# Interleaved memory attention and ReGLU: loads of two weights gated, first MLP products of two tiles joined, turns of P in either tiling

## The chip, the cores and the metric

The kernel runs on one core of one Trainium2 chip. The metric is device time in microseconds of one execution. An execution is also recorded by the hardware profiler; its own time is given beside the span that the trace shows.

## The reference, cut to what matters

Two layers, each an attention with recurrent memory and then an MLP, both added to x, both on a layer norm of x. The attention goes through 64 segments of 32 tokens in order; the first 8 rows of each segment's result are the memory that the next segment sees.

```python
def _A_ref(x, mem0, Wq, Wk, Wv, Wo, seg_len):      # S 2048, D 448, H 16, Dh 256, M 8, seg 32
    mem = mem0
    for s in range(n_seg):
        h = jnp.concatenate([mem, xs], axis=1)      # 8 rows of memory, 32 tokens
        q, k, v = h @ Wq, h @ Wk, h @ Wv            # per head
        scores = q @ k.T * scale, masked
        p = _softmax(scores, axis=-1)
        o = (p @ v) @ Wo
        mem = o[:, :M, :]
        outs.append(o[:, M:, :])
def _B_ref(x, W_gate, W_up, W_down):                # F 1792
    gate = x @ W_gate
    return (gate * (gate > 0) * (x @ W_up)) @ W_down
x = x + _A_ref(_layernorm(x), ...)
x = x + _B_ref(_layernorm(x), ...)
# the same two lines once more, with the same weights
```

## The kernel before, in words

**Folded weights.** At the start the kernel turns Wq, Wk and Wv on TensorE (`transposes`, L742 and L747) and multiplies them (`product`, L761): A holds Wq times Wk for every head, Bsb holds Wv times Wo. From then on scores are h A h and outputs are (p h) B, so no q, k or v is formed. `weights` loads Wq and Wk in four groups of heads, each group into half of eight staging slots, and behind them in the program all of Wv and Wo (`load(self.Wv_d, ...)` and the copies to `Wos`). Wv is staged in slots 8 to 15; Wo is parked in buffers that are free at the start, among them YT, hG, Ug and G2. The first two steps of the chain (`unfused`, L1039 and L1062) use Wv and Wo directly, since B isn't ready.

**The chain.** `chain(step)` is the recurrent part: the 8 memory rows of one segment of layer one and, seven steps later, of layer two, 70 steps in all. A step has products with A (L934, eight tiles of the array), scores (L1128), softmax, the turn of P, the product of P with the rows of h, called Y (L1185 and L1188), the products with B (L973, four column tiles), and a turn of the result into mT (the `Sel` products). `middle` holds scores to Y. Its probabilities P lie in Pm; those of eight-row pieces of an even tile of layer two, which ride along with the chain (66 turns), lie in Pr.

**The tiles.** The 16 tiles of 128 tokens go through `att_group` four heads at a time: products with A (L1274, two row tiles), scores (L1300), softmax, two turns of P (from Px), Y in two row tiles, and the output products (L451, untiled). That is 16 tiles in layer one and the 8 odd ones in layer two, four groups each, 96 groups. Y results wait in YT, two blocks used by turns. The MLP of a tile is `glu_units`: the first products for gate and up together (L1372), two row tiles with 64 rows each, 14 chunks of 128 hidden columns times 7 pieces of 64 rows, 128 tokens as moving columns. Gate and up stand in different PSUM banks; ScalarE writes the ReLU to hG (L1377), VectorE multiplies with up (L1378). `glu_down` makes the second products (L451, untiled) from hG, of which there is one block.

**A turn of P** before is one untiled transposition (`packed`, called in `middle` and `pt`): 128×128 in bf16 to one PSUM bank, one eviction to PT (104 rows; 128 columns in the chain, 256 for a group's two turns).

**What sets the order.** `_Sched` gives every operation an engine, a cost and a priority, and finds each one's waits. TensorE's order is fixed by the string LINE (`line`); ORDER shifts priorities of units (`part`). An operation has a mode, which is the tiling of the array: 0 untiled, 1 four column tiles, 2 two row tiles, 3 two column tiles, 4 eight tiles. An operation with `also` may take a second mode, and `line` then picks the one that its neighbours have. `room` and `alias` say which earlier users of a buffer have to be done. PSUM has eight banks in two pools. All DMAs are issued by SyncE's queue in order. Where TensorE would idle, `filler` puts spare products (L1406).

`tiles` runs at every fourth step: groups of tile t in layer one, the MLP of tile t, the MLP of tile t−4 in layer two, and groups of layer two.

Of the kernel before, what the change touches and what calls it, by code (L numbers as in the profile page):

```python
# [8 lines left out]
ALU = mybir.AluOpType  # L9
# [3 lines left out]
D = 448  # L13
# [19 lines left out]
ORDER = ("AkAPMPZMEsWPzkVtwAm0YgdLXFCHdymsALTpcTXKWNMRKLt0H0AgHAG0gihNl0bCLbZBRyVqwoWAgOvEFplk0ptQ0orawUuaBIdaABka0AA0aa"  # L33
         "UaWkSa0fNaChwaA0kcaaXrwSQNQolVYPjLmRRyjDqc0uzbiwvY0gEaaatIahC0NHXvgHbX0qAhiALw0iY0xVfRVDkaUymAt0AaAYaeCfRWpXfR"
         "lJxhempFZBlhCipGXOTk0eOorF0OaAa0faVtHTAdPi0SgiUZl0Nm0FmTRpXckrAguNAAk0TxnnA0HxlDgNSEoEVUlUXDaSSAHiaEFaPPSQjusW"
         "YsHcogi0CaBoAdNDtXVPMQkFMca0pUUVDgiUJ0xagIaPQboIbArY0SqePoFsAwfZKMgAmQsVlzU0HCASKQgeTRjtIFHqamOut0D0ya0nLcrAeT"
         "qrItxafza0hRCbp0ClsrvyAbvP0nD0EOIc0PZVUvetwAYKgbvL0w0KalaAOavpQIi0oAA0ZoAYlwmSPsLHUKDArMgzAgUELIXQA0LdqAnU0duA"
         "RSfhqzjm0kXOhRXJVfMAtVaKbaPYaKxc0G0ZSzTNpcOgMoKsBXiXfRmvsXAophduABSMYerUaaYlanAPrjhwGfrKHNc0WWgiNONAY0ZjIihT0V"
         "t0QqJhnS0LcxVbFjWBImEg0GMxNQjpxcpwkS0I0aYzavtOoz00gKAX0cLJkCaCWwVoVlVNmZ0jObxAFx00DReqAnTgacYaA0VBQTGgvXdZNTGn"
         "ixZZaanneAvXk0qXyH0tAXRAocegRGeXokpA0bAxdEZoHCsFcPcys0oFa0raAmeZcEyZQprpBkgUf00mVmuQAL0tfAtAILpMjffkzbZy0UJaXD"  # L40
         "aDgXWPdp0AXdVewhBXaIvATytDudIpyJxp0XTUswAFVsNGsiaRpOZz0ZRPojkrzZQnAfLhuKvaKXa0yCmDasEGHmoHFQXN0bYLZLTJDiANQTbR"
         "BwmtqZMtPAyNaPhavEUjupByVrFRkoAjhqSSfsUwC0AXoNBSmwAPyyXOpAcrWU0SeRJ0EpypIhQsmOFtmBji0vczampgaOqCxa0Zj0AAYMaaaa"
         "aavRbLKjCaaaaaaaaaaaaaaaaaaawkgqnN0IaIleHbO0")

SIGNS = "ABCDEFGHIJKLMNOPQRSTUVWXYZabcdefghijklmnopqrstuvwxyz0123456789+-*/=<>()[]{}.,:;!"
LINE = ("AFGEENLEGEEEFEEEMIIFGFEEFFMEM~UIJHEEEEAEDGAGECCCCCECABIIICFBECCBBKJCDCEDCBCBJJIECFDDBBJMrBIMNIAEBCECCACADBaaCC"
        "TPAnCCASCAQhAPDAONAgMBAKBAAHbHCGADaACCAAHIAVAYGBADOADCLCADJOFAHOEONEFGEBACCFBBCAAAAWAAAKARAAHOdHASAZAQXEAAAB~D"
        "AK~BAffDAC=CbAEAYEDW5WWWAAETADDRQAAANAAAKKKAJJAIAHHABFAADACAAAAAAAMSYYBAKdKbKAMR~JXAMLA~NAAAEEAHDAaaFFCCGCUABB"
        "RACPAANNNOAALANwMA1LJCJIICLHHHAGJIAAEFLAADCCAAAAABABAMAAXXQHJAaIIAQAVAAASDFDACDCbbFABADCAETAAXRABPBANNNAALANM4"
        "4MKRArKIIIBHHHAGAIHeAADEAACBBFAAAABCAATMBAXWdWKAaKhJALWuALbKAAAEJEUADDA55ElECG0ABBxBwAdCBssstAEApArqDOCAmkBBKQ"  # L50
        "hmAfVe+eeeCIdcAdcHCQAFAVVAGZAARAPIOhENNNANALMALLKcAaDIAAPGBaFZBEEEFAACKEPyxW~QEUEtAGAAPoBsnA~BDCkkkAAiiDADCgfA"
        "ADAbABBXdAAVAUAXTTTATzSBBwRQCBAAMARAAJDIAHHHKAHGBSGGdAFOTZPgOAADATNBXNBfLBBBRFFBEAAF))GqpFA/BBlF9=A8L777AA5AI5"
        "5BtBiF0AA4yDvAAttcCrrrAagEEA=FlkFlkDDhZngNACCcAbCaaaBZbAbaBFAEAVAAEQXRAPWPcDDNNNAALNKK-+aZK7ADA+4Vl2DMCzzzFAAI"
        "wvUETDssACApACtABBjADhAAfCBEcccAcAaABaZCvBWAVAAZASuSlsARRRBCAANAbhAAKAAsriiWJBBUHHAFPAREAAaABRfBL1LBBBFFBIEB))"
        "HSGACCAF+BBB7ACe4B7A222FbAAyAxzynewCAcCBGpguoTGFRkEQiiiESEEeAVcDccD7ibjAAZYsYDXXXBWABHWVHAlTAQAWgAPANUNpCMMMAA"
        "KMDIAH44UDTC0GAQA2wDD~KuTDssstAAqYEApoEDlMAAiADmAfDCdAADaaaAAYABAYXAAAUSxpZTARsRCBBANNNOAALAYACIAAGBRWdGFAPYOE"
        "AAATNBYBWgLBBBbIBEAAH{]MCCC>}RCADC-BEA8hE666AA4A55AbA2AAyCy3BwwedCVArrrGqFsrEeADPmDjDDoiRDffDKUcccfAAbaEaaHBBB"
        "VHATZAKAQAEDVNTNNNAALA//AIABGH7NG5AA3KRA000QJyACwzyDTCSuAKApDvpANnm!CCkkkAEAhDDAFAAbccDDAAAXAAVAUTnTTTATqiECBB"
        "OBAAAAYelAjXKAAIIkASRATGAACACSNCWMBdBBBFFBOEHAA))SGpF=CCCAE9LA7oDD4445AA2AA0E10ZygxAAeXtks:CvAqqqIgFBEAkADlkCF"
        "iCLmCdeCKcEaDCGXXXABVAXXUAUABSAABGOASNTMaMMMAAUJJJKQ77ff5D+AA2GB0AAyyyDAAvAxwAAKJsYpAAoHBMlk>CBiiijEAAfAAAAedA"  # L60
        "aCABBWWAAATYAStSSSAphBAAOBcAooDaAAkdApoAWvWuZJVVhHBGHGRAQPFAAACNaABMttLBBBFFJBEEBAC76DnmDAHBiy4BBwBY~LAtkDCqqq"
        "~CqVpCAAonEECkAAoBhgNAeDKcccAAbaIAaZAXOBVHFcZLSGAQqFPPPAHDMDZLNMGbKDJAAAGLTGZBFFFAAGACAAwwCVCLsFABBoCCBqEkAJii"
        "iAIPCeAgfBBbA[aaDAeAXBBVAUUUAASARTSqpZSAtQBPAOAAMMMNAAKAAdWrBBGGSmSdGGAZPFBQBDaTODNACCCGGCFCHT][ITHq<ADA*HAB=A"
        "8K7778AJA4A54dlBBA6ayAAwAvultttwuAAbrFpaoFponBFEkqEEE8hoElgYjHeeeGdfFeeE,AmHDYgZDDXPDaEUTaDWSSSAXRAYY-vEPdWAAU"
        "DMSOCQQQAERANAMDCNNAAAKIAAHFAEEADDDUADCAQBAUcGTGGRHAGBADRAEADDGAAJBOBCCBEAADCAAAAAACAAADAAAABAAAAAA")
# [1465 lines left out]
```

## Time and profile before

| | |
|---|---|
| median of 3 runs | 1504.0 us (1503.89 to 1506.61) |
| the profiled execution | 1502.79 us |
| its span | 1501.0 us |
| granted clock, mean | 0.999 |
| POOL busy | 171.7 us (11%) |
| PEld (weight loads) busy | 1059.1 us (71%) |

The span runs from the first to the last instruction of the program in the trace. PE is TensorE's products, PEld its weight loads, which overlap with them. A row of the lines view reads: line, engine, operation, what it writes and reads, shape, count | busy us, mean ns of one | idle before it and what ended that. A row of the timeline reads: start us, us, engine, line, operation, what, shape, count. Products of TensorE are pipelined, so the printed lengths overlap; the time between the starts of two rows is what the first one costs.

### The profile page before, as it was taken

To read this page: it belongs to the slowest core of one execution; us is meant where nothing else is said; L and a number is where in the kernel's file an instruction comes from. 1 tells how busy PE (TensorE), PEld (TensorE's weight loads), DVE (VectorE), ACT (ScalarE), POOL (GpSimd) and SP (SyncE) were. 2 spreads that over 40 slices of the span, in tenths; PEclk is the share of its full clock that TensorE was granted. 3 is DMA by queue.
4 is the path that set the end of the run, shared out by engine and by line. 5 is a ranking of instruction groups with operands and counts; after the bars stand their busy time and mean duration, and the time that the engine had idled before them with its cause. 6 is when DMAs were issued, how large, how long until landed. Compare 5 with 4: busy or idle time off the path is not lost.

```text
span 1501.0 us, 83432 instructions
## 1 busy us (share of the span) xinstructions
PE 1482.8 (99%) x37128; PEld 1059.1 (71%) x37128; DVE 1144.8 (76%) x3528; ACT 909.7 (61%) x2539; POOL 171.7 (11%) x669
## 2 busy tenths in 40 slices
PE   8999999999999999999999999999999999999999
PEld 6557566676767777777768677777768776677776
DVE  6657678787777878688878877688777877778765
ACT  6776566666666666555565656565665665565543
POOL 3010111111111111011110111011110011111000
PEclk9999999999999999999999999999999999999999
DMA  9602100000000000000000000000000000000000
GB/s 231 184 25 66 54 7 12 11 9 8 9 4 12 11 8 15 4 17 6 17 6 12 11 9 14 3 18 5 18 5 8 14 9 14 4 10 6 12 5 15
DMA packets 62262, 34.12 MB, mean 23 GB/s; under 512 B 31552, under 2 KB 61776, under 8 KB 61904
## 3 DMA queue, kind: packets, MB, share of 16 engines
q1 hardware_dynamic: 61904, 28.80, 8.1%
q8 instruction: 292, 4.78, 1.4%
q14 instruction: 66, 0.54, 0.1%
HBM read 21.36 MB, written 1.84 MB: 15 GB/s over the span
## 4 chain that ended last, share of the span: by engine, by line
PE 94%; DVE 2%; ACT 1%; DMA 1%; issue 1%; SPq 0%; POOL 0%; DVEq 0%
PE psG L451 24%; PE psG L1274 17%; PE psG L1372 12%; PE psC L973 11%; PE psC L934 9%; PE psG L934 4%; PE psG L1185 3%; PE psG L761 3%; PE psG L1300 2%; PE psC L451 2%; PE psC L1128 2%; PE psC L1185 1%; PE psG L973 1%; PE psG L1188 1%; DMA Bsb<-in_A_Wq_dram 1%
## 5 line engine op out<-in xcount | busy, mean ns | idle before, releaser
L1274 PE MATMUL psG<-HT,A 64*128 64x128 bf16 x4980 | 288.9, 216 | 1.2 <-issue 1.2
L451 PE MATMUL psG<-Bsb,YT 128*128 128x448 bf16 x1288 | 274.6, 352 | 0.0
L1274 PE MATMUL psG<-HX,A 64*128 64x128 bf16 x3735 | 269.6, 216 | 0.5 <-issue 0.3
L1274 PEld LDWEIGHTS psG<-HT,A 64*128 64x128 bf16 x4980 | 236.5, 94 | 13.6 <-issue 4.2
L441 ACT ACTIVATE Ug<-psG 64x128 bf16<-64x128 f32 (+2 forms) x442 | 156.6, 374 | 68.5 <-PE psG L1274 56.6
L1274 PEld LDWEIGHTS psG<-HX,A 64*128 64x128 bf16 x3735 | 195.5, 94 | 0.8 <-issue 0.8
L1372 PE MATMUL psG<-G,glu 64*128 64x128 bf16 x5950 | 190.7, 216 | 1.2 <-issue 0.9
L1372 PEld LDWEIGHTS psG<-G,glu 64*128 64x128 bf16 x5950 | 175.4, 94 | 13.6 <-issue 6.2
L451 PEld LDWEIGHTS psG<-Bsb,YT 128*128 128x128 bf16 x1288 | 113.0, 97 | 95.7 <-issue 10.0
L973 PE MATMUL psC<-Bsb,YTm 128*32 128x448 bf16 x3416 | 172.9, 353 | 0.4
L1112 DVE STREAM_TRANSPOSE uT<-Usb 128x384 bf16<-128x384 bf16 x280 | 154.0, 551 | 0.8
L934 PE MATMUL psG<-A,mT 64*32 64x448 bf16 x4032 | 152.5, 350 | 0.0
L934 PE MATMUL psC<-A,mT 64*32 64x448 bf16 x3808 | 147.3, 350 | 0.5 <-ACT mT L441 0.5
L973 PEld LDWEIGHTS psC<-Bsb,YTm 128*32 128x32 bf16 x3416 | 85.5, 97 | 67.0 <-DVE YTm L444 1.6
L441 ACT ACTIVATE YT<-psG 128x448 bf16<-128x448 f32 x233 | 118.8, 543 | 10.6 <-PE psG L1188 9.1
L444 DVE CAST Ug<-psG 64x128 bf16<-64x128 f32 (+2 forms) x254 | 108.1, 438 | 16.9 <-PE psG L1274 12.9
L934 PEld LDWEIGHTS psC<-A,mT 64*32 64x32 bf16 x3808 | 76.0, 92 | 53.4 <-ACT mT L441 5.2
L1377 ACT ACTIVATE hG<-psG 128x512 bf16<-128x512 f32 (+1 forms) x127 | 69.0, 543 | 63.2 <-PE psG L1372 58.0
L451 PE MATMUL psG<-glu,hG 128*128 128x448 bf16 x448 | 99.3, 352 | 0.0
L934 PEld LDWEIGHTS psG<-A,mT 64*32 64x32 bf16 x4032 | 80.1, 92 | 19.8 <-DVE mT L444 0.7
L1378 DVE TENSOR_TENSOR hG<-hG,psG 128x512 bf16<-128x512 bf16 (+1 forms) x116 | 70.5, 613 | 29.2 <-ACT hG L1377 28.3
L444 DVE CAST YT<-psG 128x448 bf16<-128x448 f32 x136 | 82.0, 616 | 9.5 <-PE psG L1188 8.1
(235 smaller groups left out, 2856.9 us busy)
## 6 DMA issues: line engine op xcount, KB each, us to landing
HR<-xn SPq DMA_DIRECT2D x128, 32.0 KB
Tsb<-Rsb SPq DMA_DIRECT2D x256, 1.5 KB
Tsb<-Rsb SPq DMA_DIRECT2D x256, 2.0 KB
Bsb<-in_A_Wk_dram SPq DMA_DIRECT2D x6, 448.0 KB
Bsb<-in_A_Wq_dram SPq DMA_DIRECT2D x6, 448.0 KB
HR<-Rsb SPq DMA_DIRECT2D x126, 1.5 KB
HR<-Rsb SPq DMA_DIRECT2D x126, 2.0 KB
X<-in_A_x_dram SPq DMA_DIRECT2D x16, 112.0 KB
```

The source lines that it names most:

```text
L441: return E.activation(out, i, ACT.Copy, scale=1.0 if scale is None else scale)
L444: return E.tensor_copy(out, i)
L451: return E.matmul(out, lhsT=lhsT, rhs=rhs, **k)
L761: i = E.matmul(bk.ap()[row0:row0 + mn, to:to + of.stop - of.start], lhsT=lhs[:, et, m0:m0 + mn], rhs=rhs[:, et, of], start=(et == 0), stop ...
L934: i = E.matmul(ub[v].ap()[32 * j:32 * j + 32, 0:D], lhsT=self.mT[rw, WHERE[b], first:first + 32], rhs=cols, start=(b == 0), stop=(b == 6), ...
L973: x = E.matmul(bo.ap()[32 * j:32 * j + 32, 0:D], lhsT=self.YTm[:, q, :], rhs=self.Bsb[:, chunks[q], :], start=(i == 0), stop=(i == 13), ti ...
L1112: self.s.add("dve", 578, lambda E, e, out=out, hh=hh: E.transpose(out, heads[hh]), r=[("Usb", 2 * half + v) for v in range(2)], w=[f"uT{ha ...
L1185: return E.matmul(ps[:, n * q:n * q + n], lhsT=HR[rows, 128 * q:128 * q + 128], rhs=PT, start=True, stop=True, tile_position=(b, 0))
L1274: i = E.matmul(ub[v].ap()[:, 128 * n:128 * n + 128], lhsT=self.A[rw, b, a0:a0 + 128], rhs=HT[rw, WHOLE[b], :, 0:SEG] if CROSS[b] is None e ...
L1372: i_ = E.matmul(two[v].ap()[:, 128 * c:128 * c + 128], lhsT=self.Wgu[rw, b, f0:f0 + 128], rhs=G[rw, WHOLE[b] if CROSS[b] is None else 4 + ...
L1377: s.add("act", 170 + 0.833 * N, lambda E, e, dst=dst, z=two[0], N=N: E.activation(dst, z.ap()[:, 0:N], ACT.Relu), r=[two[0]], w=[("hG", i, ...
L1378: s.add("dve", dv_cost(N), lambda E, e, z=two[1], N=N, dst=dst: E.tensor_tensor(dst, dst, z.ap()[:, 0:N], ALU.mult), r=[two[1]], w=[("hG", ...
```

## The change

It has three parts, and new strings ORDER and LINE.

1. Every load of Wv and Wo now reads a key that the 16th `transposes` writes. These are the turns of the first and the second group of heads of Wq and Wk.
2. From tile 4 on, `glu_units` takes two tiles together, t of layer one and t−4 of layer two. Their normalized inputs lie side by side in GG; a product has 256 moving columns in two stretches of 128; a unit is two chunks, of which there are seven. YT (two blocks) and hG (one block) become one buffer P3 with three blocks. `take` hands out the block that was handed out longest ago, and its earlier users are waited for. Both tiles' second products follow, then the groups of layer two that came ahead of them before.
3. A turn of P is now a product with the identity, not a transposition in TensorE's own sense: fp32 results in two banks of 64 columns each, untiled (two products of 64 columns) or as two row tiles (one product in each), whichever its neighbours in TensorE's order have. There are two evictions, one from each bank.

```diff
+def turned(E, mode, banks, at, P, ident):
+    for v in range(2):
+        rw = slice(64 * v, 64 * v + 64)
+        out = banks[v].ap()
+        if mode == 2:
+            i = E.matmul(out[:, at:at + 64], lhsT=P[rw, :], rhs=ident[rw, rw], start=True, stop=True, tile_position=(64 * v, 0))
...
+        else:
+            i = E.matmul(out[:, at:at + 64], lhsT=P, rhs=ident[:, rw], start=True, stop=True)
+    return i
...
-NYT = 2
-NHG = 1
+NSH = 3
...
+    def take(self, parts):
+        i = self.turns.pop(0)
+        self.turns.append(i)
+        old = self.held[i]
+        self.epoch[i] += 1
+        self.held[i] = [("P3", i, self.epoch[i], q) for q in range(parts)]
+        return i, old, self.held[i]
...
             self.dma(self.Wst[slot][:, 0:3, :], src[64:448, c0:c0 + 512].rearrange("(k p) c -> p k c", p=128), 393216,
-                     w=[("Wst", slot)])
+                     r=[("turned", 16)], w=[("Wst", slot)])
...
-        bp = self.bank("C", "G")
-        s.add("pe", 56, lambda E, e: packed(E, e, bp.ap().bitcast(BF)[:, 0:128], m["P"][:, :], self.ident[:, :], is_transpose=True),
-              r=[k_("P"), k_("P0"), k_("P1"), "ident"], w=[bp], alloc=[bp], **P)
-        s.add(EV, ev_cost(128, fast=True), copy_any(m["PT"][0:104, :], lambda: bp.ap().bitcast(BF)[0:104, 0:128]), r=[bp], w=[k_("PT")], **P)
+        bp = [self.bank("C", "G") for _ in range(2)]
+        s.add("pe", 56, lambda E, e: turned(E, e, bp, 0, m["P"][:, :], self.ident),
+              r=[k_("P"), k_("P0"), k_("P1"), "ident"], w=bp, alloc=bp, also=(2,), **P)
+        for v in range(2):
+            s.add(EV, ev_cost(64), copy_any(m["PT"][0:104, 64 * v:64 * v + 64], lambda v=v: bp[v].ap()[0:104, 0:64]), r=[bp[v]], w=[k_(f"PT{v}")], **P)
...
+        if len(tg) == 2:
+            (i, old, ka), (j, old2, kb) = sorted((self.take(7), self.take(7)), key=lambda x: x[0])
+            old = old + old2
+            for k in range(7):
+                s.part()
+                two = [self.bank("G", "C") for _ in range(2)]
+                def fn(E, e, two=two, k=k):
+                    for c in range(2):
+                        f0 = 128 * (2 * k + c)
+                        for b in range(7):
+                            for v in range(2):
+                                rw = slice(64 * v, 64 * v + 64)
+                                i_ = E.matmul(two[v].ap()[:, 256 * c:256 * c + 256], lhsT=self.Wgu[rw, b, f0:f0 + 128],
+                                              rhs=self.GG[rw, :, WHOLE[b] if CROSS[b] is None else 4 + CROSS[b], :],
+                                              start=(b == 0), stop=(b == 6), tile_position=(64 * v, 0))
...
+        if 4 <= t < NT:
+            s.now = step + 4
+            for x in self.glu_units([(t, g1), (t - 4, g4)]):
+                self.glu_down(*x)
+            self.store(t - 4)
+            first()
```

More of the change, by code (lines that the diff above doesn't have):

```diff
@@ L456, in packed @@
     return i
+def turned(E, mode, banks, at, P, ident):
[4 more added lines that the diff above has]
+            i = E.matmul(out[:, at:at + 64], lhsT=P[rw, :], rhs=ident[rw, rw], start=True, stop=True, tile_position=(64 * v, 0))
+        elif mode == 1:
+            for j in range(4):
+                q = slice(32 * j, 32 * j + 32)
+                i = E.matmul(out[q, at:at + 64], lhsT=P[:, q], rhs=ident[:, rw], start=True, stop=True, tile_position=(0, 32 * j))
+        else:
+            i = E.matmul(out[:, at:at + 64], lhsT=P, rhs=ident[:, rw], start=True, stop=True)
+    return i
 def bass_interleave_layers__memory_aug_recurrent_mem_tr__glu_gated_reglu__prompt_kernel(
@@ L627, in alloc @@
         self.Ug = [sb(f"Ug{i}", [128, 4, 4, 128]) for i in range(NUG)]
-        self.YT = [sb(f"YT{i}", [128, 14, 128]) for i in range(NYT)]
-        self.hG = [sb(f"hG{i}", [128, NFC, 128]) for i in range(NHG)]
+        self.P3 = sb("P3", [128, NSH, 14, 128])
+        self.turns = list(range(NSH))
+        self.epoch = [0] * NSH
+        self.held = [[("P3", i, 0)] for i in range(NSH)]
         self.psum = {n: self.ps(f"ps{n}", [128, 512]) for p in self.s.pools.values() for n in p}
@@ L748, in fn @@
                 return i
-            s.add("pe", mm_cost(*[128 if slot >= 8 else 112] * 8), fn, r=keys + ["ident"], w=[bk], alloc=[bk], room=[("WT", wt)])
+            s.add("pe", mm_cost(*[128 if slot >= 8 else 112] * 8), fn, r=keys + ["ident"], w=[bk, ("turned", turn[0])], alloc=[bk], room=[("WT", wt)])
             s.add(EV, ev_cost(896, fast=True), copy_any(T.rearrange("p a b -> p (a b)"), lambda: bk.ap().bitcast(BF)[:, base:base + 896]),
@@ L1313, in att_group @@
         s.add("dve", dv_cost(160), lambda E, e: E.tensor_tensor(P[:, :, 0:L], T[:, :, :], bc(rc), ALU.mult), r=[k_("Tx"), k_("rc")], w=[("Px", si)])
-        bp = self.bank("G", "C")
+        bp = [self.bank("G", "C") for _ in range(2)]
         Pf = P[:, :, :].rearrange("p g k -> p (g k)")
@@ L1335, in att_group @@
             hk = [q for h in range(2) for q in self.hr_keys(l, 4 * t + 2 * p + h)]
-            s.add("pe", mm_cost(*[128] * 3, 64, 64), yy, r=["PTx"] + hk, w=yb, alloc=yb, room=[("YT", yi, p, h) for h in range(2)], mode=2)
+            s.add("pe", mm_cost(*[128] * 3, 64, 64), yy, r=[("PTx", 0), ("PTx", 1)] + hk, w=yb, alloc=yb, room=old, mode=2)
             for h in range(2):
@@ L1384, in glu_down @@
         bk = self.bank("G", "C")
-        hG = self.hG[i]
+        hG = self.P3[:, i]
         for q in range(4):
```

169 lines of the change are left out of this document (98 added, 71 removed).

## The prediction

> **What bounds the kernel now.** I read the page first: the engines' busy shares, the row of granted clocks, and the chain that ended last.
>
> ```profile
> span 1501.0 us, 83432 instructions
> PE 1482.8 (99%) x37128; PEld 1059.1 (71%) x37128; DVE 1144.8 (76%) x3528; ACT 909.7 (61%) x2539; POOL 171.7 (11%) x669
> PE 94%; DVE 2%; ACT 1%; DMA 1%; issue 1%; SPq 0%; POOL 0%; DVEq 0%
> ```
>
> TensorE is busy for 99% of the span and makes up 94% of the chain. The windows view says where it is not.
>
> ```profile
> 0.00:37.50 37.50, 32.15 (x471) 23.04 (x471) 25.70 (x60) 24.62 (x39) 12.13 (x43) 1.00 1.05 231
> 37.50:75.00 37.50, 35.27 (x531) 21.68 (x533) 22.61 (x45) 26.52 (x48) 2.95 (x6) 0.95 0.63 184
> 100.00:300.00 200.00, 195.59 (x4896) 133.03 (x4896) 146.59 (x455) 124.03 (x348) 25.09 (x95) 1.00 0.12 31
> 300.00:1200.00 900.00, 897.91 (x23302) 653.32 (x23299) 712.69 (x2256) 548.70 (x1602) 101.40 (x403) 1.00 0.05 10
> ```
>
> The columns after the length are the busy times of PE, PEld, DVE, ACT and POOL, then granted clock, DMA share and GB/s. From 300 to 1200 us TensorE lacks 2.1 us of 900. At the start it lacks 5.4 and 2.2 us, while the DMA engines move 231 GB/s. So the time changes only with what stands in TensorE's queue, and with stalls of the start. What a product costs there I read from the times between starts in the timeline, since the printed durations overlap.
>
> ```profile
> 602.25 0.28 PE L451 MATMUL psG<-ident,Px 128*128 128x128 bf16 x2
> 602.36 0.22 PE L451 MATMUL psG<-ident,Pm 128*128 128x128 bf16 x1
> 602.42 2.06 PE L451 MATMUL psG<-Bsb,YT 128*128 128x448 bf16 x10
> 604.41 0.34 PE L1185 MATMUL psC<-PTm,HR 40*128 40x128 bf16 x6
> 604.58 0.22 PE L1188 MATMUL psC<-PTm,HR 40*128 40x64 bf16 x4
> 604.64 0.33 PE L1185 MATMUL psG<-PTx,HR 40*128 40x128 bf16 x6
> ...
> 605.04 0.22 PE L1188 MATMUL psG<-PTx,HR 40*128 40x64 bf16 x4
> 605.19 0.57 PE L1300 MATMUL psG<-HT,Ug 128*128 128x40 bf16 x16
> ```
> ```profile
> 226.85 0.23 PE L451 MATMUL psC<-ident,Pm 128*128 128x128 bf16 x1
> 227.01 0.23 PE L1185 MATMUL psC<-PTr,HR 40*128 40x128 bf16 x1
> ```
> ```profile
> 1489.65 5.65 PE L1372 MATMUL psG<-G,glu 64*128 64x128 bf16 x196
> 1495.23 2.82 PE L451 MATMUL psG<-glu,hG 128*128 128x448 bf16 x14
> ```
>
> Two untiled turns of P take 0.11 us, 0.055 each. Four products of 64 columns in row tiles (604.58 to 604.64) take 0.06, which is 0.028 for a pair that runs side by side. A turn that stands alone between row-tiled products needs 0.16 (226.85 to 227.01): 0.055 for itself and 0.105 for **the change of tiling** behind it. 605.04 to 605.19 says the same for the way back: 0.15 less two pairs is 0.095. So an untiled stretch between two row-tiled ones costs 0.20 us beyond its products. In all I count 595 changes of tiling, the last at 1495.23 above and the first here:
>
> ```profile
> 10.74 2.91 PE L761 MATMUL psG<-glu 128*64 128x384 bf16 x56
> ```
>
> At about 0.1 each these are some 60 us, more than all idle time.
>
> **First MLP products in 256 columns.** A tile's 98 pairs (1489.65 to 1495.23) take 5.58 less 0.105, so 55.9 ns a pair of 128 columns. An untiled product of 448 columns takes (1.99 − 0.105)/10 = 188.5 ns. The line through both is 0.4144 ns a column and 2.9 ns a product. Two tiles together therefore save one 2.9 for each pair of products that becomes one. Tiles 4 to 15 of the first layer are joined with tiles 0 to 11 of the second: 12 × 98 × 2.9 ns = **3.4 us**. Bounds 0 (the fixed part grows with the second stretch that the operand is read from) and 3.4; I take 3.4, since the 448 columns stream at that rate from one start to the next. The evictions lie beside TensorE's work: seven of 512 columns for two tiles instead of six of 512 and two of 256.
>
> **Turns of P.** 96 groups with two turns, 70 steps and 66 riders make 328 turns; these rows hold 312 of them, and smaller groups hold the rest:
>
> ```profile
> L451 PE MATMUL psG<-ident,Px 128*128 128x128 bf16 x190 | 26.2, 219 | 0.0
> L451 PE MATMUL psC<-ident,Pm 128*128 128x128 bf16 x63 | 13.9, 221 | 0.2
> L451 PE MATMUL psC<-ident,Pr 128*128 128x128 bf16 x59 | 13.0, 220 | 0.1
> ```
>
> As row tiles a turn takes 28 ns, 27 less than now. Untiled it becomes two products of 64 columns, 2 × (64 × 0.4144 + 2.9) = 59 ns, 4 more. So the ends are 328 × 27 = 8.9 us gained and 328 × 4 = 1.3 lost. The share in row tiles isn't in the trace; it is set by the new order. I take 0.6, nearer the good end, because the products that consume a turn are row-tiled and because a turn needs only a neighbour of that kind: 197 × 27 − 131 × 4 = **4.8 us**.
>
> A turn that needs no untiled stretch can also make one unnecessary. I count 103 untiled stretches between row-tiled ones; 14 hold turns but no scores, from 120.5 to 1473.8 us. None gone is one bound. Half of the 103 gone (52 × 0.20 = 10.4 us) is the other, since scores and output products must still be untiled somewhere. I take 20, a little over the 14: **4.0 us**.
>
> The price is evictions: two of fp32, one bank each, in place of one of bf16.
>
> ```profile
> L441 ACT ACTIVATE PTx<-psG 104x256 bf16<-104x256 bf16 x70 | 26.8, 383 | 16.3 <-PE psG L451 15.8
> L444 DVE COPY PTx<-psG 104x256 bf16<-104x256 bf16 x25 | 7.2, 287 | 6.3 <-PE psG L451 6.2
> L441 ACT ACTIVATE PTm<-psC 104x128 bf16<-104x128 bf16 x50 | 13.8, 276 | 32.5 <-PE psC L451 32.2
> L441 ACT ACTIVATE mC<-psC 128x128 bf16<-128x128 f32 x54 | 15.0, 277 | 1.7
> L444 DVE CAST mC<-psC 128x128 bf16<-128x128 f32 x13 | 3.8, 292 | 0.4
> L996 DVE CAST mT<-psC 128x64 bf16<-128x64 f32 x67 | 14.8, 222 | 23.4 <-PE psC L451 23.2
> ```
>
> A group pays 277 + 292 instead of 383 or 287: about 210 ns more (74% were on ACT). A chain turn pays about 2 × 222 instead of 276: 170 more. Together 96 × 0.21 + 136 × 0.17 = 43 us over two engines that idle 356 and 591 us. That idle time and TensorE's other products hide it, except where TensorE has nothing else to do than wait for the chain. That is the case from 100 to 300 us, where it lacks 4.4 us. If both evictions of a chain turn stand on one engine, its 10 steps there pay 0.17 each. Bounds: below nothing, 10 × 0.05 when both engines share it (222 against 276); above, all 70 steps, 12 us. I take **2.3 us lost**, 1.7 for these ten and the rest for the second bank, which each turn now holds out of eight.
>
> **Loads behind the 16th weight turn.**
>
> ```profile
> 15.96 2.84 PE L761 MATMUL psG<-glu 128*64 128x448 bf16 x28
> 25.38 0.95 PE L742 MATMUL psG<-ident,Bsb 112*128 112x112 bf16 x16
> 39.25 0.90 PE L742 MATMUL psG<-ident,Bsb 112*128 112x112 bf16 x8 [2.50 <-issue]
> 40.19 3.91 PE L761 MATMUL psG<-glu 128*64 128x448 bf16 x28
> 48.95 1.07 PE L747 MATMUL psG<-ident,Bsb 128*128 128x128 bf16 x16
> ```
> ```profile
> 13.05 5.35 SPq L706 DMA_DIRECT2D Bsb<-in_A_Wv_dram  x3
> ...
> 58.89 0.38 SPq L706 DMA_DIRECT2D G<-in_A_Wo_dram  x1
> ```
>
> The 16th turn ends at 26.3 us (25.38 + 0.95). Only the first Wv load, 448 KB, was issued before that, and it held SP's queue for 5.35 us, with later Wk loads behind it. At 231 GB/s it is 2.0 us of the DMA engines. Later TensorE stood for 2.50 us ahead of a turn of Wq or Wk; the clock came down (0.95 in that window), so 28 products took 3.91 instead of 2.84. These 3.6 us can go. On the other side all Wv and Wo, 7.3 MB, now start at 26 us, beside 1.8 MB of the last Wq and Wk: 40 us at 231 GB/s and 50 at the second window's 184, so until 66 or 76, where the last was issued at 58.89 before. The waiting loads also hold back in SP's queue the loads of X and the copies to HR that are issued after them. The first Wv was needed at 48.95. Bounds: 3.6 gained, 15 lost (76 less 61, which is 58.89 and an estimated 2 us for the transfer); I take **2.0 gained**, the first load's own DMA time, since TensorE's order can be put behind the loads.
>
> **The sum:** −3.4 − 4.8 − 4.0 + 2.3 − 2.0 = −11.9 us. The profiled execution took 1502.8 us (span 1501.0 and 1.8 around it), the median of the runs shown is 1504.0, so it stands 0.08% below. 1502.8 − 11.9 = **1491 us**.
>
> **Rivals.**
>
> *The turns stay untiled and the start gains nothing*: the order may use the freedom nowhere. Then −3.4 + 1.3 + 2.3 = 0.2, so 1503. For it: every untiled turn quoted above sits beside untiled products, where it costs no change of tiling. Against: a row tile also halves the turn itself.
>
> *Blocks of the shared buffer* (the slower side). Before, Y results had two blocks and the hidden values one, each for itself. Now a joined MLP takes two of three blocks from its first products to its last second products: 98 × 109 ns + 2 × 14 × 188.5 ns = 16 us, and more with other work between, out of some 80 us for four steps. Meanwhile groups have one block: a group's Y can't be evicted before the group ahead has been read, and its output products stand in TensorE's queue behind that eviction.
>
> ```profile
> L441 ACT ACTIVATE YT<-psG 128x448 bf16<-128x448 f32 x233 | 118.8, 543 | 10.6 <-PE psG L1188 9.1
> ```
>
> A wait is one eviction, 0.54 us, and it outweighs the gain once over 22 of the 96 groups pay it. If 45 do, 45 × 0.54 = 24 us are lost: 1515. Against: TensorE's order can put MLP products in between.
>
> *Wv and Wo come too late* for the first steps, which use them unfused: 15 us lost instead of 2.0 gained, 1508. For it: the second window's 184 GB/s. Against: only 448 KB of the 7.3 MB were ahead of that point before.
>
> *Weight loads pace the row-tiled products.* Then halving them for 24 of 32 tiles would save far more than 2.9 ns each.
>
> ```profile
> L1372 PEld LDWEIGHTS psG<-G,glu 64*128 64x128 bf16 x5950 | 175.4, 94 | 13.6 <-issue 6.2
> ```
>
> That would be 175.4 × 0.75 / 2 = 66 us, 1437. The 55.9 ns a pair speak against it: 128 columns at 0.4144 are 53.0 of them. The Trainium skill, page "TensorE: Matmul & The Clock Gate", section "Back-to-back issue gap", says that weight load and product together set the pace, 81 ns a product at 128 columns and 131 at 512. By that, estimated from the page, 256 columns would cost about 97 instead of 162, some 76 us less in all; 5.58 us for 98 pairs disagree.
>
> *The evictions* are the rule that speaks against this change: the Trainium skill, page "TensorEngine Tiling (Array Packing)", section "PSUM Bottleneck", warns that once tiling has sped up TensorE, copying PSUM out may bind. ACT at 61% and DVE at 76% leave room for 43 us; by the rule the loss would go to the 12 us bound above.
>
> **How the numbers follow.** About 0.2% (3 us) is what a measurement of this kernel can tell from no change. The forecast, 1478 to 1500, gets 0.66. More than that gets 0.07: 1476 is nearly all good ends together (3.4 + 8.9 + 10.4 + 3.6 = 26 us), and 0.01 of it is the pace of weight loads. Little or no gain, 1500 to 1507, gets 0.11, blocks 0.11 and late loads 0.05. Faster: 0.66 + 0.07 + 0.02 from the edge of the third = 0.75; same 0.09; slower 0.16. The range 1476 to 1508 leaves out the blocks' 0.11, half of the late loads and little below, under 0.2 in all.
>
> **What would show it.** Right: 98 products of the joined MLP about 10.7 us a pair of tiles; most turns as 64×128 products with 64 columns; fewer than 560 changes of tiling; no gap of 2.5 us near 39 us. Wrong: gaps on TensorE that end with ACT or DVE writing the shared buffer or PT, more changes of tiling than 595, or waits for Wv or Wo before 75 us.

## The result, and the profile after

| | before | after |
|---|---|---|
| median of the runs timed together (4 each) | 1505.3 us | 1493.6 us |
| range of these runs | 1503.9 to 1506.6 | 1492.8 to 1495.8 |
| ratio, with its 95% interval | | 0.9931 [0.9909, 0.9952] |
| the profiled execution | 1502.79 us | 1495.75 us |
| its span | 1501.0 us | 1494.0 us |

By the ratio the changed kernel is faster by 10.4 us, with an interval of 7.2 to 13.7; the two medians differ by 11.7. The two profiled executions differ by only 7.0 us: the one of before lies 2.5 us under its median, the one of after 2.1 us over its own. So the traces are used for where the time lies, the timed runs for how much it is.

The same lines of the page, after:

```profile
span 1494.0 us, 79650 instructions
PE 1478.5 (99%) x35088; PEld 1042.1 (70%) x35088; DVE 1151.2 (77%) x3627; ACT 917.0 (61%) x2648; POOL 172.0 (12%) x669
PE 95%; DVE 2%; ACT 1%; DMA 1%; issue 0%; SPq 0%; POOL 0%; DVEq 0%
```

TensorE still bounds the kernel, with 2040 products fewer. ACT and DVE carry 208 instructions more, the second evictions among them, and are as far from full as before. The windows view, in the same stretches as before (length, then busy time of PE, PEld, DVE, ACT and POOL, then granted clock, DMA share, GB/s):

```profile
0.00:37.50 37.50, 33.16 (x449) 23.04 (x450) 23.53 (x53) 23.47 (x39) 13.74 (x44) 0.95 1.06 224
37.50:75.00 37.50, 35.82 (x563) 22.13 (x561) 22.73 (x52) 29.58 (x53) 1.42 (x5) 1.00 0.64 192
100.00:300.00 200.00, 196.37 (x5037) 135.31 (x5043) 147.94 (x476) 124.33 (x368) 23.91 (x92) 1.00 0.12 32
300.00:1200.00 900.00, 897.92 (x21783) 640.56 (x21769) 716.54 (x2302) 560.62 (x1694) 103.55 (x411) 1.00 0.05 10
```

From 300 to 1200 us TensorE lacks 2.08 us of 900, as before. The second stretch keeps its clock (1.00 for 0.95), the first has lost some (0.95 for 1.00). The timeline of TensorE in the changed kernel (start us, us, engine, line, operation, what, shape, count):

```profile
120.31 0.22 PE L1305 MATMUL psG<-HT,A 64*128 64x128 bf16 x2
120.36 0.19 PE L465 MATMUL psC<-ident,Pm 64*128 64x64 bf16 x2
120.39 0.22 PE L1305 MATMUL psG<-HT,A 64*128 64x128 bf16 x2
...
609.11 0.28 PE L471 MATMUL psG<-ident,Px 128*128 128x64 bf16 x4
609.23 0.18 PE L451 MATMUL psC<-Sel,Ohi 128*128 128x32 bf16 x1
...
625.36 10.87 PE L1408 MATMUL psG<-GG,glu 64*128 64x256 bf16 x196
636.17 0.19 PE L451 MATMUL psC<-Sel,Ohi 128*128 128x32 bf16 x1
```

A row-tiled turn takes 0.03 us from its start to the next row's, with no change of tiling on either side. Two untiled turns take 0.12 (609.11 to 609.23), and stand between untiled products. 98 pairs of 256 columns take 10.81 us to the next row. Less one change of tiling that is 10.7, as forecast.

TensorE's time falls into parts when each product is given a price: those that the prediction worked out, and for a pair of 256 columns and for the shortest products what the timeline shows (109.2 and 25 ns). So all but the rest are counts times prices. All other products are the same 30483 in both kernels, and their price doesn't touch the differences. "Rest" is what is left between TensorE's first and last product, changes of tiling and gaps; 4.2 us of each span lie ahead of the first and behind the last.

| profiled execution | first MLP products | turns of P | spare products | all other products | rest | changes of tiling |
|---|---|---|---|---|---|---|
| before | 175.1 | 18.3 | 5.3 | 1204.2 | 93.9 | 595 |
| after | 172.2 | 16.3 | 3.6 | 1204.2 | 93.5 | 598 |

So 7.0 us of the profiled pair are 2.9 from the 256 columns, 2.0 from the turns, 1.7 from spare products (29 for 45, 11 of the 16 before 75 us) and 0.4 from the rest. Changes of tiling aren't fewer. The rows of the turns in the lines view (busy us, mean ns of one | idle before) show how many are row-tiled, L465, and how many not, L471:

```profile
L471 PE MATMUL psG<-ident,Px 128*128 128x64 bf16 x268 | 18.7, 192 | 0.0
L471 PE MATMUL psC<-ident,Pm 128*128 128x64 bf16 x87 | 10.6, 194 | 0.1
L465 PE MATMUL psG<-ident,Px 64*128 64x64 bf16 x114 | 6.7, 190 | 0.0
L465 PE MATMUL psC<-ident,Pr 64*128 64x64 bf16 x30 | 4.1, 192 | 0.2 <-issue 0.2
```

Two products make a turn. Over all such rows 194 products, 97 turns, are row-tiled and 231 turns are not: a share of 0.30. Of the 231, 184 stand inside an untiled stretch, so that they cost no change of tiling where they are.

The start, TensorE's timeline first and then SyncE's:

```profile
39.08 0.81 PE L770 MATMUL psG<-ident,Bsb 112*128 112x112 bf16 x13 [0.32 <-issue]
39.83 2.84 PE L789 MATMUL psG<-glu 128*64 128x448 bf16 x28
...
53.58 1.52 PE L965 MATMUL psC<-A,mT 64*32 64x448 bf16 x56 [0.24 <-DVE A L443]
```
```profile
30.04 0.58 SPq L733 DMA_DIRECT2D Bsb<-in_A_Wk_dram  x1
30.66 1.72 SPq L733 DMA_DIRECT2D Bsb<-in_A_Wv_dram  x3
...
56.04 1.17 SPq L733 DMA_DIRECT2D GG<-in_A_Wo_dram  x1
```

The last Wk is now issued ahead of the first Wv. In these two executions the gap near 39 us is 0.32 us in place of 2.50, the 28 products behind it take 2.84 in place of 3.91, and the first product of the chain (the 64*32 product of A with mT) starts at 53.58. Before it started here:

```profile
57.55 1.52 PE L934 MATMUL psC<-A,mT 64*32 64x448 bf16 x56
```

Of these 4.0 us only 0.7 are left at the chain's second step, so the first product alone doesn't say what the chain gains.

### The profile page after: what moved, and what is told of

The parts are those of the page before. It is cut to its first block, busy times and chain, and to the rows that moved or that the text cites. A ratio compares the mean times of both kernels' runs of the same rounds, so it can differ in the third digit from the quotient of the medians.

```text
span 1494.0 us, 79650 instructions
## 1 busy us (share of the span) xinstructions
PE 1478.5 (99%) x35088; PEld 1042.1 (70%) x35088; DVE 1151.2 (77%) x3627; ACT 917.0 (61%) x2648; POOL 172.0 (12%) x669
## 4 chain that ended last, share of the span: by engine, by line
PE 95%; DVE 2%; ACT 1%; DMA 1%; issue 0%; SPq 0%; POOL 0%; DVEq 0%
PE psG L451 22%; PE psG L1305 16%; PE psC L1004 11%; PE psG L1408 9%; PE psC L965 8%; PE psG L965 4%; PE psC L451 3%; PE psG L1217 3%; PE psG L789 3%; PE psG L1331 3%; PE psG L1437 3%; PE psG L1004 2%; PE psC L1159 1%; PE psC L1217 1%; PE psG L1220 1%; PE psC L1305 1%
## 5 line engine op out<-in xcount | busy, mean ns | idle before, releaser
L451 PE MATMUL psG<-Bsb,P 128*128 128x448 bf16 x1176 | 250.6, 353 | 0.0
L451 PEld LDWEIGHTS psG<-Bsb,P 128*128 128x128 bf16 x1176 | 102.0, 97 | 88.7 <-issue 10.0
L965 PE MATMUL psC<-A,mT 64*32 64x448 bf16 x3696 | 138.0, 350 | 0.5 <-DVE A L443 0.2
L1408 PE MATMUL psG<-GG,glu 64*128 64x256 bf16 x2338 | 135.3, 269 | 0.0
L441 ACT ACTIVATE P<-psG 128x448 bf16<-128x448 f32 x243 | 122.1, 544 | 11.2 <-PE psG L1220 9.2
L1408 PEld LDWEIGHTS psG<-GG,glu 64*128 64x128 bf16 x2338 | 111.5, 94 | 17.6 <-issue 2.2
L444 DVE CAST Ug<-psG 64x128 bf16<-64x128 f32 (+2 forms) x237 | 99.0, 426 | 13.7 <-PE psG L1305 8.5
L451 PE MATMUL psG<-glu,P 128*128 128x448 bf16 x434 | 94.9, 352 | 0.0
L444 DVE CAST P<-psG 128x448 bf16<-128x448 f32 x126 | 76.3, 613 | 17.2 <-PE psG L1220 15.6
L1418 ACT ACTIVATE P<-psG 128x512 bf16<-128x512 f32 x84 | 50.1, 596 | 59.9 <-PE psG L1408 53.9
L1419 DVE TENSOR_TENSOR P<-P,psG 128x512 bf16<-128x512 bf16 x83 | 56.6, 682 | 36.1 <-ACT P L1418 35.5
```

The lines of the kernel that those rows point to most:

```text
L441: return E.activation(out, i, ACT.Copy, scale=1.0 if scale is None else scale)
L444: return E.tensor_copy(out, i)
L451: return E.matmul(out, lhsT=lhsT, rhs=rhs, **k)
L965: i = E.matmul(ub[v].ap()[32 * j:32 * j + 32, 0:D], lhsT=self.mT[rw, WHERE[b], first:first + 32], rhs=cols, start=(b == 0), stop=(b == 6), ...
L1408: i_ = E.matmul(two[v].ap()[:, 256 * c:256 * c + 256], lhsT=self.Wgu[rw, b, f0:f0 + 128], rhs=self.GG[rw, :, WHOLE[b] if CROSS[b] is None ...
L1418: s.add("act", ev_cost(512)["act"], lambda E, e, dst=dst, z=z: E.activation(dst, z(0), ACT.Relu), r=[two[0]], w=w, room=old)
```

## The experiments

The theory: TensorE's queue sets the time, so each part is worth the products and changes of tiling that it takes out, and the gate (the wait of the loads of Wv and Wo for the 16th turn) is worth the time that the start loses without it. The rivals: weight loads set the pace of row-tiled products; evictions and PSUM banks bind; the order of work, not the operations, is what pays. Each ratio is to the kernel before on the same chip, with its 95% interval; a difference of two ratios is given in us of 1503, with the square root of the sum of their squared half widths.

**The changed kernel again** (e1_same), nothing edited.

> The changed kernel itself, as the measure for the other three of this call. Theory (parts): 7 to 12 us under the kernel before; in the trace first products 2.9 us less of TensorE, turns of P 2.0 less, about 600 changes of tiling as before (595), the rest from the start. Rival (start): all but 3 us of the gain comes from the loads. Rival (order): most of the gain comes from the turns in row tiles, which let the order save changes of tiling. This run says how large the gain is that the others divide.

Median 1492.9 us, 0.9935 [0.9919, 0.9951], span 1492.7, 598 changes. The gain is there again, and this is the base for what follows. In this execution the chain starts at 50.57 us, 3.0 earlier than above, and the span is 1.3 shorter: not all that the start gains is kept.

**Without the gate** (e2_ungated).

```diff
-                     r=[("turned", 16)], w=[("Wst", slot)])
+                     w=[("Wst", slot)])
```

(So also at the other loads of Wv and Wo.)

> The changed kernel, loads of Wv and Wo without the wait for the 16th turn. Theory (parts): 2 to 4 us slower than the changed kernel, with a gap of over 1 us on TensorE before 45 us and a first chain step near 57 us instead of 53.6. Rival (start): 8 us or more slower, nearly the kernel before. Rival (order): within 1 us of the changed kernel.

1529.3 us, 1.0170 [1.0152, 1.0189]: 35 ± 4 us slower than the changed kernel, ten times what the theory said. SyncE's timeline, then TensorE's:

```profile
7.58 2.36 SPq L733 DMA_DIRECT2D Bsb<-in_A_Wv_dram  x3
...
57.36 0.58 SPq L733 DMA_DIRECT2D Bsb<-in_A_Wk_dram  x1
```
```profile
80.36 1.52 PE L965 MATMUL psC<-A,mT 64*32 64x448 bf16 x56 [0.24 <-DVE A L443]
```

Ungated, loads of Wv and Wo go between those of Wk and Wq all the way to 57 us, and the chain starts 27 us later than in the first trace of the changed kernel. TensorE does spare products meanwhile, 482 of them here, in the lines view:

```profile
L1473 PE MATMUL psC<-ident 128*128 128x128 bf16 x482 | 27.6, 219 | 0.0
```

Against e1_same, where the chain starts at 50.57 us, the first step is 29.8 us behind, the sixth 31.6, and the last 30.5. So the whole loss is the start's. The old order had ungated loads too and started its chain at 57.55 us; the loss is that of the new order without its gate.

**Turns untiled** (e3_untiled_turns).

```diff
-              r=[k_("P"), k_("P0"), k_("P1"), "ident"], w=bp, alloc=bp, also=(2,), **P)
+              r=[k_("P"), k_("P0"), k_("P1"), "ident"], w=bp, alloc=bp, **P)
```

(And the same at a group's turns.)

> The changed kernel with every turn of P untiled, in the same order. 97 of 328 turns stood in row tiles. Theory (parts): each costs 59 instead of 28 ns, 3.0 us, and each of some 65 units that held them inside a row-tiled stretch costs two changes of tiling, up to 13 us: 8 to 16 us slower than the changed kernel, 650 to 730 changes of tiling. Rival (start): under 4 us slower. Rival (order): as the theory or more; the two are told apart by the turns alone in the kernel before.

1509.0 us, 1.0045 [1.0028, 1.0063]: 16.5 ± 3.6 us slower than the changed kernel. In spans it is 15.3: products 3.2 (19.1 for 16.3 in the turns, 0.4 spare), rest 12.1 (104.3 for 92.2), with 697 changes of tiling for 598. 99 changes at 0.1 are 9.9 of that. One turn in the timeline, first with the turns untiled, then in the changed kernel:

```profile
1402.75 2.83 PE L1004 MATMUL psC<-Bsb,YTm 128*32 128x448 bf16 x56
1405.51 0.20 PE L471 MATMUL psC<-ident,Pr 128*128 128x64 bf16 x1
1405.55 0.19 PE L471 MATMUL psG<-ident,Pr 128*128 128x64 bf16 x1
1405.68 0.34 PE L1217 MATMUL psG<-PTx,HR 40*128 40x128 bf16 x6
```
```profile
1389.65 2.83 PE L1004 MATMUL psC<-Bsb,YTm 128*32 128x448 bf16 x56
1392.42 0.20 PE L465 MATMUL psC<-ident,Pr 64*128 64x64 bf16 x1
1392.42 0.20 PE L465 MATMUL psG<-ident,Pr 64*128 64x64 bf16 x1
1392.45 0.33 PE L1217 MATMUL psG<-PTx,HR 40*128 40x128 bf16 x6
```

Untiled, the turn takes 0.17 us up to the products that follow; as row tiles 0.03. The 0.14 are 0.03 of the turn and one change of tiling. This shows the mechanism: a turn as row tiles takes a change of tiling away where its neighbours are tiled. It shows too that the new order needs it: without it that order has 102 changes more than before had.

**128 columns** (e4_128_columns), each joined product in two again.

```diff
-                                i_ = E.matmul(two[v].ap()[:, 256 * c:256 * c + 256], lhsT=self.Wgu[rw, b, f0:f0 + 128],
+                                    a0 = 256 * c + 128 * h
+                                    i_ = E.matmul(two[v].ap()[:, a0:a0 + 128], lhsT=self.Wgu[rw, b, f0:f0 + 128],
...
```

> The changed kernel, joined first MLP products made as two of 128 columns, 1176 more pairs of products and as many more weight loads. Theory (parts): 2.5 to 2.9 ns for each pair, 2.9 to 3.4 us slower than the changed kernel. Rival: the two stretches of the operand cost as much as they save, 0. Weight loads set the pace: over 20 us slower.

1498.5 us, 0.9968 [0.9956, 0.9981]: 5.0 ± 3.0 us slower than the changed kernel, 3.0 in spans. The same tiles' products in its timeline:

```profile
622.89 11.12 PE L1410 MATMUL psG<-GG,glu 64*128 64x128 bf16 x392
633.94 0.19 PE L451 MATMUL psC<-Sel,Ohi 128*128 128x32 bf16 x1
```

11.05 us for 10.81, so 0.24 a pair of tiles and 2.9 for twelve. Twice the weight loads cost no more than that; they don't set the pace.

**The gate alone** (e5_before_gated): the kernel before, with the loads of Wv and Wo behind the 16th turn.

```diff
-                     w=[("Wst", slot)])
+                     r=[("turned", 16)], w=[("Wst", slot)])
...
-            s.add("pe", mm_cost(*[128 if slot >= 8 else 112] * 8), fn, r=keys + ["ident"], w=[bk], alloc=[bk], room=[("WT", wt)])
+            s.add("pe", mm_cost(*[128 if slot >= 8 else 112] * 8), fn, r=keys + ["ident"], w=[bk, ("turned", turn[0])], alloc=[bk], room=[("WT", wt)])
```

> The kernel before with the gate alone: loads of Wv and Wo wait for the 16th turn, its own order. Theory (parts): 2.0 us faster than the kernel before, bounds 3.6 faster and 15 slower; the gap of 2.5 us near 39 us gone. Rival (start): 5 us or more faster. Rival (late loads): slower, with waits for Wv or Wo before 75 us.

1499.3 us, 0.9972 [0.9962, 0.9982]: 4.2 us faster, between 2.7 and 5.7; 3.3 in spans. SyncE's timeline and then TensorE's:

```profile
26.91 2.07 SPq L706 DMA_DIRECT2D Bsb<-in_A_Wk_dram  x1
29.02 3.10 SPq L706 DMA_DIRECT2D Bsb<-in_A_Wv_dram  x3
```
```profile
37.88 0.55 PE L743 MATMUL psG<-ident,Bsb 112*128 112x112 bf16 x8 [0.23 <-issue]
...
38.42 2.84 PE L762 MATMUL psG<-glu 128*64 128x448 bf16 x28
...
55.94 1.52 PE L935 MATMUL psC<-A,mT 64*32 64x448 bf16 x56
```

In this trace the gap near 39 us and the lower clock of before are gone (a gap of 1.25 us stands before 35.41 us instead), and the chain starts 1.6 us earlier. The trace of e10_before_first_gated below shows much the same without the gate, so that the 4.2 us rest on the timed runs alone. The last Wk is issued 2.6 us earlier than in the trace of before, which has it here:

```profile
29.49 0.61 SPq L706 DMA_DIRECT2D Bsb<-in_A_Wk_dram  x1
```

But two other ungated traces of the old order have it at 26.95 and 27.10 us (e6_before_turned and e7_before_turned_untiled).

Measured by itself in the old order, the gate is worth more than the 2.9 and the 2.0 us of products that the other two parts take out.

**The new turns alone** (e6_before_turned): the kernel before with turns of either tiling, two banks and two evictions, its strings LINE and ORDER as they were. The diff is that of the turns in the section on the change.

> The kernel before with the turns of P alone, untiled or as row tiles by their neighbours in the old order, two banks, two evictions. 35 turns follow row-tiled products directly and 5 stand alone, so some 40 get row tiles: 40 x 27 ns gained, 288 x 4 ns lost, up to 10 changes of tiling (1 us) gone, evictions 2.3 us lost. Theory (parts): within 3 us of the kernel before. Rival (order): the same, since the old order can't use it. Rival (evictions bind): 8 us or more slower.

1512.7 us, 1.0066 [1.0052, 1.0080]: 9.9 us slower, where the theory said within 3. Its 588 changes are 7 fewer than before; only 40 turns of 328 are row-tiled; the rest is 101.6 us for 93.9.

**The same, untiled** (e7_before_turned_untiled): as above without `also=(2,)`.

> The kernel before with the new turns, all untiled: two products of 64 columns, two banks, two evictions each. Theory (parts): 1.3 us for TensorE and 2.3 us for evictions, 3.6 us slower than the kernel before (bounds 1 and 13). Rival (evictions bind): 10 us or more slower, with gaps on TensorE behind PTx, PTm or PTr.

1517.3 us, 1.0086 [1.0071, 1.0101]: 12.9 us slower. Turns are 0.8 us longer, changes as before (595), the rest 104.3. So 10.4 us more lie between the products, with no more changes of tiling: in the old order the second eviction and the second bank cost time (e9_before_one_bank below takes them back).

**The old turn in the new order** (e8_after_old_turn): the changed kernel with the transposition, one bank and one eviction of before.

```diff
-        bp = [self.bank("C", "G") for _ in range(2)]
+        bp = self.bank("C", "G")
...
-        for v in range(2):
-            s.add(EV, ev_cost(64), copy_any(m["PT"][0:104, 64 * v:64 * v + 64], lambda v=v: bp[v].ap()[0:104, 0:64]), r=[bp[v]], w=[k_(f"PT{v}")], **P)
+        s.add(EV, ev_cost(128, fast=True), copy_any(m["PT"][0:104, :], lambda: bp.ap().bitcast(BF)[0:104, 0:128]), r=[bp], w=[k_("PT0"), k_("PT1")], **P)
```

> The changed kernel with the turns of before (transposition in bf16, untiled, one bank, one eviction) in its new order. Against the same order with new untiled turns (15 us slower than the changed kernel) it lacks only the second product and the second eviction. Theory (parts): 3.6 us better than that, so 11 to 12 us slower than the changed kernel, with about 697 changes of tiling. Rival (evictions bind): 10 us or more better than that, within 5 us of the changed kernel.

1511.3 us, 1.0055 [1.0042, 1.0067]: 18.0 ± 3.1 us slower than the changed kernel. Beside the untiled new turns in the same order (e3_untiled_turns, 1.0045, 697 changes there too) it differs by 1.5 ± 3.3. So in the new order giving up the second bank and the second eviction brings nothing that can be measured, while in the old one adding them cost some 10 us. The run is also 8.3 us slower than the kernel before (6.3 to 10.1), though it has the gate and the 256 columns: the new order alone, without the new turns, doesn't pay.

**One bank in the old order** (e9_before_one_bank): two fp32 products of 64 columns a turn, untiled, into one bank, one eviction.

```diff
+def turned(E, out, at, P, ident):
+    for v in range(2):
+        i = E.matmul(out[:, at + 64 * v:at + 64 * v + 64], lhsT=P, rhs=ident[:, 64 * v:64 * v + 64], start=True, stop=True)
+    return i
...
```

> The kernel before, turns of P as two untiled products of 64 columns (fp32) but into one bank and with one eviction. The same with two banks and two evictions was 12.9 us slower than the kernel before. Theory (second bank and second eviction cost the rest): 1 to 4 us slower than the kernel before, 1.3 of it TensorE's. Rival (fp32 evictions or the products themselves): 9 us or more slower.

1505.1 us, 1.0016 [1.0004, 1.0028]: 2.4 us slower than before, and 10.5 ± 2.9 faster than with two banks and two evictions (e7_before_turned_untiled). The windows view, from 600 us on, first with two banks, then with one:

```profile
600.00:900.00 300.00, 297.19 (x7672) 217.10 (x7677) 237.94 (x758) 174.66 (x535) 32.80 (x132) 1.00 0.05 10
900.00:1200.00 300.00, 298.92 (x7794) 219.54 (x7774) 233.97 (x746) 182.53 (x546) 32.42 (x128) 1.00 0.05 11
1200.00:1513.00 313.00, 307.56 (x7747) 222.25 (x7745) 233.68 (x739) 171.31 (x504) 27.15 (x110) 1.00 0.04 9
```
```profile
600.00:900.00 300.00, 299.46 (x7842) 220.24 (x7841) 237.44 (x742) 175.55 (x515) 33.40 (x134) 1.00 0.05 10
900.00:1200.00 300.00, 299.85 (x7770) 220.15 (x7772) 233.69 (x737) 181.65 (x531) 31.11 (x123) 1.00 0.05 11
1200.00:1502.40 302.40, 298.98 (x7583) 216.60 (x7575) 223.06 (x683) 166.80 (x466) 27.35 (x111) 1.00 0.04 9
```

TensorE's idle time there is 2.81 + 1.08 + 5.44 = 9.3 us with two and 0.54 + 0.15 + 3.42 = 4.1 with one, while ACT and DVE are no busier than 80% in any of these stretches. So their load as a whole doesn't explain it. The waits view says what ended TensorE's longer gaps from 600 us on: with two banks 15 gaps of 5.6 us in all, with one bank 2 of 0.7. Two rows with two banks (what waited, what ended it, us in all, times, longest):

```profile
PE psG L471 <- DVE Px L1330: 1.0, 1, 1.0
PE psC L1391 <- ACT PTm L441: 0.3, 1, 0.3
```

The second is the only one of the 15 that ends with the eviction of a turn, though such gaps were expected with two banks. The others end with other work, mostly of ACT and DVE. So the second bank and eviction make other results late; by what path isn't shown, and these runs don't tell the bank and the eviction apart.

**One load gated** (e10_before_first_gated): the kernel before with only the load of staging slot 8 behind the 16th turn.

```diff
-                     w=[("Wst", slot)])
+                     r=[("turned", 16)] if slot == 8 else [], w=[("Wst", slot)])
```

> The kernel before, only the first Wv load (448 KB, issued at 13 us) waits for the 16th turn; the other loads are left as they were. With all of Wv and Wo gated it was 4.2 us faster. Theory (that one load stood in front of Wk): 3 to 5 us faster than the kernel before, no gap over 1 us on TensorE between 30 and 45 us. Rival (the order of all the other loads matters): less than 1.5 us faster.

1502.6 us, 0.9999 [0.9986, 1.0013]. A miss in its design: the Wv load that stands at 13.05 us before is that of slot 9, so the order of loads stayed as it was. Its trace is still of use. With the loads in the order of before, its profiled span is 1497.3 us:

```profile
37.66 0.55 PE L743 MATMUL psG<-ident,Bsb 112*128 112x112 bf16 x8 [1.19 <-ACT glu L441]
...
38.20 2.84 PE L762 MATMUL psG<-glu 128*64 128x448 bf16 x28
...
54.49 1.52 PE L935 MATMUL psC<-A,mT 64*32 64x448 bf16 x56
```

The gap is 1.19 us, not 2.50, the 28 products take 2.84, not 3.91, and the chain starts 3.1 us earlier than in the trace of before, and even 1.4 earlier than with all loads gated (55.94). So two traces of the start can differ by 3 us without any change of the loads, and what one trace gains there can't be put down to the gate.

**The gate at the 8th turn** (e11_gate_8), the changed kernel.

```diff
-                     r=[("turned", 16)], w=[("Wst", slot)])
+                     r=[("turned", 8)], w=[("Wst", slot)])
```

> The changed kernel with the gate at the 8th turn (end of the first heads' turns) instead of the 16th, in its own order. Then about 1.8 MB of Wv and Wo go out ahead of the last Wk of the second heads' group and of the third group's loads. Theory (each load ahead costs its transfer, 4 us for 0.9 MB at 231 GB/s): 4 to 8 us slower than the changed kernel, against 26 of filler products and 36 in all without a gate. Rival (any gate does): within 2 us of the changed kernel.

1502.4 us, 0.9993 [0.9984, 1.0003]: 8.7 ± 2.8 us slower than the changed kernel, a little over the 4 to 8 expected. SyncE's timeline:

```profile
23.15 4.33 SPq L733 DMA_DIRECT2D Bsb<-in_A_Wv_dram  x3
28.15 0.50 SPq L733 DMA_DIRECT2D Bsb<-in_A_Wk_dram  x1
...
34.09 0.58 SPq L733 DMA_DIRECT2D Bsb<-in_A_Wk_dram  x1
```

The last Wk leaves at 34.09 us, where in the changed kernel it left at 30.04 in one trace and at 27.20 in the other (e1_same). The chain starts at 57.30, and in those at 53.58 and 50.57. With no gate it was 57.36 and 80.36. Over all eight traces of the new order the chain starts 20.9 to 23.5 us after the last Wk is issued, whether that is at 27 us or at 57. So there each load ahead of the second heads' Wk delays the chain. Against e1_same this run is 6.7 us behind at the first step and 7.2 from the sixth on. In the six traces of the old order the distance is 25.2 to 29.6 us.

**Turns at the end of an untiled stretch as row tiles** (e12_tail), the changed kernel with this in `line`.

```diff
+        for o, p in zip(out[-2::-1], out[:0:-1]):
+            if p.mode in o.also:
+                o.mode = p.mode
```

> The changed kernel; a turn of P that ends an untiled stretch ahead of a row-tiled one is made as row tiles with the stretch behind it. 22 turns of the 231 untiled ones stand so. Theory (parts): 22 x 31 ns = 0.7 us faster, about 598 changes of tiling as before. Rival (order and evictions hang together): the shifted change of tiling moves evictions to other engines and banks, and it is 2 us or more slower in spite of less work for TensorE.

1497.3 us, 0.9958 [0.9944, 0.9971]: 3.5 ± 3.1 us slower than the changed kernel, where 0.7 faster was expected. 240 products are now row-tiled for 194 and the turns take 15.6 us for 16.3, yet its profiled span of 1494.4 us is no shorter than the 1494.0 and 1492.7 of the changed kernel: the rest is 93.7 us (93.5 and 92.2), and spare products take 4.6 for 3.6. So 0.7 us of TensorE's products don't reach the end. What else makes it slower the trace doesn't show, and the interval only just leaves out no difference.

No version beat the changed kernel.

## Why the prediction was right, and where it was not

The forecast was 1491 us; it came to 1493.6. That the sum came so near is in good part luck. The turns and the stretches were forecast at 8.8 us together, and the products of the turns gave 2.0, with no fewer changes of tiling; against these 6.8 us stand 2.3 us of evictions that can't be measured in the new order, and a gate worth 2.2 us more than forecast.

- *What bounds the kernel.* Right. TensorE's queue sets the time, before and after, and the products that the parts take out show up there.
- *256 columns, 3.4 us.* Right: 2.9 by the traces (172.2 for 175.1), 5.0 ± 3.0 timed. The price of 2.9 ns a product holds: two pairs of 128 were 112 ns, one of 256 is 109.2 (10.7 us by 98). Weight loads as the pace, with its 66 us, is refuted. So is the estimate of 97 ns for 256 columns in place of 162 for two of 128, worked out from the Trainium skill, page "TensorE: Matmul & The Clock Gate", section "Back-to-back issue gap": the trace has 109.2 in place of 112.
- *The price of a change of tiling, 0.1 us.* Right as far as it is shown: 99 more changes with untiled turns come with 12.1 us more in the rest, 0.12 each, gaps included.
- **The step that failed:** "A turn that needs no untiled stretch can also make one unnecessary", taken as 20 stretches and 4.0 us. There are 598 changes, not under 560. Counted in the two traces, the untiled stretches between row-tiled ones did fall, from 103 to 92, and those that hold turns but no scores from 14 to 1. But untiled stretches beside other tilings rose from 118 to 131, so that all untiled ones are 223 for 221. The mechanism exists: within the new order row tiles for the turns are worth 16.5 us, 3.2 of them products. But that order has 102 changes more than the old one if its turns are untiled. The freedom was spent on another order, and did not lower the count. What that other order gained for it isn't shown: in the table the rest is the same within 0.4 us. The count of stretches was read from the old order, and the term leaves out what a new order does with all the others.
- *Share of row-tiled turns, 0.6.* Wrong: 0.30. By the prediction's own prices 97 × 27 − 231 × 4 = 1.7 us; the traces give 2.0, not 4.8. That "the products that consume a turn are row-tiled" was no reason: 184 of the 231 stand inside untiled stretches, where an untiled turn is cheap.
- *Evictions and banks, 2.3 us lost.* Not borne out in either order. In the old one they cost about 10 us (12.9 with two banks, 2.4 with one), near the 12 of the rival. In the new one taking them back should have gained 2.3 us, and 0.8 of products, and came out 1.5 ± 3.3 slower. The Trainium skill, page "TensorEngine Tiling (Array Packing)", section "PSUM Bottleneck", warns that copying out of PSUM may become the bottleneck once tiling has sped TensorE up. Neither order shows that: the old one lost its 10 us with untiled turns, ACT at 60% and DVE at 77%, and the new one lost nothing that can be measured. The prediction priced an eviction by the engines' idle time, and e7_before_turned_untiled shows that time is lost beside idle engines; the path by which it is lost stays open.
- *Loads behind the 16th turn, 2.0 us.* Right in its direction, too small: 4.2 [2.7, 5.7]. It counted one load's DMA time. The bound of 3.6 lies nearer, but not by its reason: the gap and the lower clock that it adds up are smaller or gone in e10_before_first_gated with the loads in the order of before. That loads of Wv in SP's queue hold back those of Wk, and these the chain, is shown in the new order: with no gate the last Wk leaves 30 us later than in e1_same, and so does the chain. How the 4.2 us of the old order come about isn't shown.
- *Blocks of the shared buffer.* No run changes the number of blocks, so this is not shown by experiment. The traces speak against it: from 300 to 1200 us TensorE lacks 2.08 us after and 2.09 before.
- *Wv and Wo too late.* Refuted: the last Wo is issued at 56.04 us (58.89 before), where the loads were feared to last until 66 or 76, and the chain starts earlier than before.

The three parts together: 4.2 for the gate (measured in the old order), 2.9 for the columns and 2.0 for the turns are 9.1 us, against 10.4 [7.2, 13.7] measured. The 1.3 between them is less than these runs can tell. But this adds up products, and doesn't say that each part would pay by itself. By the runs the new turns cost 9.9 us in the old order and bring 18.0 in the new one, which without them is slower than the old.

Open: what e12_tail's 3.5 us are made of; why the old turn in the new order isn't faster than the untiled new one, although its products take 0.8 us less; and how much of the start's gain, which differs by some us from one execution to the next, reaches the end.

## What to carry to other kernels

Where one engine's queue is written out by hand, price an edit in the order that it will run in: the same second bank and eviction cost 10 us in one order and nothing that can be measured in another, and the same gate 4 us in one and 35 in the other. Before forecasting fewer changes of tiling, ask what the new order will buy with the freedom; the count may come back as it was. And order the loads of one queue by when they are needed, since loads ahead of their turn held back here all that stood behind them, by 30 us where none was gated.

## What the runs showed of the hardware

A stream of row-tiled products whose weights change every time runs at 0.4144 ns a column and 2.9 ns a product at both 128 and 256 columns (11.05 and 10.81 us for the same 98 × 256 columns), so twice the weight loads cost no more than that fixed part (0.24 us for 98, 2.4 ns each). Two row tiles of 64 columns in two banks run side by side in 0.03 us (1392.42 to 1392.45). And the start of one and the same program differs between executions: the chain began at 53.58 us in one and at 50.57 in another, with the loads in the same order, and a granted clock of 0.95 and 1.00 in the first 37.5 us; in both it began 23.4 to 23.5 us after the last load of Wk was issued.
